# Scores and the packed projection as float32 matmuls on 64x32 array tiles instead of block-diagonal 128-row matmuls

## The chip, the cores and the metric

The kernel runs on one core of one Trainium2 chip. The core has a matrix engine (TensorE, PE in the profile, with its weight loads shown apart as PEld), a vector engine (VectorE, DVE), a scalar engine (ScalarE, ACT), a general engine (GpSimd, POOL) and a queue engine that here only starts DMAs (SyncE, SP). They work in parallel and wait for each other through semaphores. Matrix results land in PSUM, an accumulator memory of which the kernel uses eight banks and from which ScalarE and VectorE read them; operands lie in SBUF, both of 128 partitions. The metric is the device time of one execution in microseconds (us). Three runs of the kernel before took 1118.48, 1119.23 and 1120.44 us; the median is 1119.23.

## The reference

The reference first packs each head's sequence with 32 learned queries, attends to the packed result, and puts the output through two dense blocks. Cut to what matters (4 batches, 8 heads, 576 positions, head size 64, 32 packed positions):

```python
def sm_attn(qq, kk, vv):                       # softmax(qq kk^T / 8) vv
    s = scale * np.matmul(qq, kk.transpose(0, 1, 3, 2))
    a = np.exp(s - np.max(s, axis=-1, keepdims=True))
    return np.matmul(a / (np.sum(a, axis=-1, keepdims=True) + 1e-09), vv)

p_packed = sm_attn(p, k, v)                    # 32 rows for each head
x = sm_attn(q, p_packed, p_packed)             # heads side by side: 2304 x 512
for e in range(4):                             # w1[e] 512x1024, w2[e] 1024x512
    out += prob[:, e:e+1] * (np.maximum(x @ w1[e], 0.0) @ w2[e])
h = out @ w_in                                 # w_in 512x2048, float64
return (h - np.tanh(h)) @ w_out                # w_out 2048x512, float64
```

## The kernel before

The work runs in two phases. Phase A is the attention and the first mixture; phase B, from about 690 us, is the second dense block and is not touched by the change. Tokens are handled in two halves p = 0, 1 of two batches each (nine tiles of 128 tokens), and the mixture in eight chunks c of 512 hidden columns.

Large products are kept accurate by splitting an operand x into a rounded high part and the rest, both of type fp32r, and adding three matmuls (high by high, high by low, low by high). A plain float32 matmul needs no split. Both kinds are used.

The stages have letters, and the order in which the program creates them is written out by hand in the strings START_A, START_B (the start and chunk 0), EVEN, ODD and LAST (the later chunks). From that order and its own estimates a scheduler makes the order of each engine.

- K, V, L load k, v and q of a batch. S (`pack_scores`, L157) makes the scores of the 32 packed queries of two head pairs against all 576 keys, and the softmax. Two heads share the 128 rows of the array: `pbd` holds the packed queries block-diagonally, each pair as 128x64 with zeros in the off-diagonal blocks, so one float32 matmul on a 64-column strip gives two heads. T (L183) transposes the probabilities, P (`pack_pv`, L195) multiplies them with v and copies the result, 32 packed rows a head, into a block-diagonal buffer `ppbd` (eight copies of 64x32 a batch). Z splits `ppbd` into `pph` and `ppl`.
- Q (`q_scores`, L221) makes the scores of two token tiles against the packed rows, again with a block-diagonal operand, then a softmax in groups of 32: maximum (qmx), subtraction, exponential (ScalarE), sum (qsm), two small steps, multiplication. X (`q_T`, L261) transposes the probabilities and splits them into `a2h` and `a2l`.
- W (`pack_w1`, L348) is the packed projection. Instead of applying the probabilities to the packed rows and then w1, the packed rows are multiplied with a chunk of w1 first, and the probabilities are applied to that. Each call takes two head pairs: six fp32r matmuls (L355) of 512 columns from the splits of `ppbd` and of w1, then three ScalarE passes (`wph`, L365) and three VectorE passes (`wpl`, L368). There are 4 calls a chunk, 32 in all. The tile w1 is staged by `a0`, split by `b0` (`w1h`, `w1l`, L341).
- u (`up`, L374; the accumulator is hps) applies the probabilities to that product, with the ReLU; d (`down`, L405; yps) multiplies with w2 and adds the weighted result to x. An underscore decodes a piece of the float64 weights of phase B in the background.

The accumulators come from two pools: `ps2`, two buffers of two banks, used by S, T, W, u and later by phase B, and `ps1`, four buffers of one bank, used by P, Q, X and d. A stage that needs a buffer waits until the engines that read the stage before it in that buffer are done.

## Time and profile before

| | before |
|---|---|
| median of three runs, us | 1119.23 (1118.48 to 1120.44) |
| span of the profiled execution, us | 1116.0 |
| TensorE busy, of the span | 1097.5 us (98%) |
| VectorE busy | 766.3 us (69%) |
| ScalarE busy | 521.0 us (47%) |
| GpSimd busy | 11.9 us (1%) |
| chain that ended last | PE 97%, DVE 2% |
| share of W on that chain | 4% |
| shares of pv, sc, qsc on it | 1% each |

The profile shows one execution. The span goes from its first to its last instruction; its own time outside of that is not listed apart, and the median of the runs is 3.2 us longer than the span. Busy times are of instructions, so a matmul counts from its start to the modelled end of its last column, and successive ones overlap: what one costs in a stream is the distance between two starts, not its duration. A float32 matmul appears as two instructions, an fp32r matmul as one. The chain that ended last is followed back from the last instruction, at each step to what released it.

### The profile page before, as it was taken

How to read it: one execution, taken by the hardware profiler on the slowest of the kernel's cores; microseconds unless marked ns; L12 is line 12 of the kernel's file. 1: busy time of each engine (PE TensorE's matmuls, PEld its weight loads, DVE VectorE, ACT ScalarE, POOL GpSimd, SP SyncE). 2: the span in 40 equal slices, each digit the busy share in tenths (PEclk: the TensorE clock that was granted, in tenths of full speed). 3: DMA queues.
4: the chain of work that ended last, by engine and by line, in shares of the span. 5: the costliest groups of instructions: out<-in, count | busy, mean ns of one | idle time of the engine just before them, and what ended most of it. 6: DMA issues, size and time to landing. Idle time of an engine off the chain costs nothing.

```text
span 1116.0 us, 14894 instructions
## 1 busy us (share of the span) xinstructions
PE 1097.5 (98%) x6100; PEld 937.7 (84%) x6100; DVE 766.3 (69%) x1055; ACT 521.0 (47%) x743; POOL 11.9 (1%) x13
## 2 busy tenths in 40 slices
PE   7799999999999999999999999999999999999998
PEld 5688888898888888888889888888888888888887
DVE  5937456876876776867787544487676767777775
ACT  3535533433434433443434322476666556556463
POOL 2100000000000000000000000000000000000000
PEclk9999999999999999999999999999999999999999
DMA  9620202322331331332322031201011262202102
GB/s 341 227 86 1 76 22 93 114 95 76 113 113 66 114 124 57 115 112 84 107 95 95 19 145 64 95 1 38 1 38 38 74 228 95 76 1 76 57 19 76
DMA packets 33668, 96.68 MB, mean 87 GB/s; under 512 B 3776, under 2 KB 3776, under 8 KB 33600
## 3 DMA queue, kind: packets, MB, share of 16 engines
q1 hardware_dynamic: 33600, 95.73, 24.6%
q8 instruction: 48, 0.79, 0.3%
q14 instruction: 20, 0.16, 0.0%
HBM read 69.51 MB, written 26.21 MB: 86 GB/s over the span
## 4 chain that ended last, share of the span: by engine, by line
PE 97%; DVE 2%; ACT 0%; DMA 0%; issue 0%; DVEq 0%; SPq 0%; ACTq 0%
PE yps L413 35%; PE hps L387 18%; PE ops L626 18%; PE h3ps L570 18%; PE wps L355 4%; PE pv L205 1%; PE sc L162 1%; PE xps L448 1%; PE qsc L235 1%; DVE wpl L368 0%; PE tp L188 0%; PE qtp L268 0%; DMA kt<-in_kT_dram 0%; DVE mx L168 0%; DVE pn L464 0%
## 5 line engine op out<-in xcount | busy, mean ns | idle before, releaser
L413 PE MATMUL yps<-w2h,hm 128*128 128x512 f32 x640 | 206.2, 391 | 0.0
L570 PE MATMUL h3ps<-xh,ws 128*128 128x512 f32 (+1 forms) x640 | 187.3, 368 | 0.0
L626 PE MATMUL ops<-ws,gh 128*128 128x512 f32 x576 | 177.2, 396 | 0.0
L413 PE MATMUL yps<-w2h,hu 128*128 128x512 f32 x512 | 165.0, 392 | 0.0
L387 PE MATMUL hps<-a2h,wph 128*128 128x256 f32 (+1 forms) x512 | 151.3, 296 | 2.5 <-DVE wpl L368 1.7
L387 PE MATMUL hps<-a2l,wph 128*128 128x256 f32 (+1 forms) x512 | 151.5, 296 | 1.0 <-DVE a2l L272 1.0
L387 PE MATMUL hps<-a2h,wpl 128*128 128x256 f32 (+1 forms) x512 | 151.3, 296 | 0.0
L413 PEld LDWEIGHTS yps<-w2h,hm 128*128 128x128 f32 x640 | 119.8, 188 | 23.5
L570 PEld LDWEIGHTS h3ps<-xh,ws 128*128 128x128 f32 x640 | 116.5, 188 | 20.6
L626 PEld LDWEIGHTS ops<-ws,gh 128*128 128x128 f32 x576 | 107.6, 189 | 24.2 <-ACT gh L605 0.2
L413 PE MATMUL yps<-w2l,hm 128*128 128x512 f32 x320 | 125.1, 391 | 0.0
L424 DVE SCALAR_TENSOR_TENSOR x<-yps,pn,x 128x512 f32<-128x512 f32 x126 | 93.7, 747 | 37.7 <-PE yps L413 36.5
L570 PE MATMUL h3ps<-xl,ws 128*128 128x512 f32 (+1 forms) x320 | 117.7, 368 | 0.0
L397 DVE SCALAR_TENSOR_TENSOR hm<-hps,hm 128x640 fp32r<-128x640 f32 x64 | 52.7, 823 | 85.7 <-ACT hm L396 85.3
L626 PE MATMUL ops<-ws,gl 128*128 128x512 f32 x288 | 109.7, 395 | 0.0
L413 PEld LDWEIGHTS yps<-w2h,hu 128*128 128x128 f32 x512 | 94.5, 188 | 16.9
L396 ACT ACTIVATE hm<-hps 128x640 fp32r<-128x640 f32 x64 | 45.1, 705 | 135.4 <-PE hps L387 135.2
L387 PEld LDWEIGHTS hps<-a2h,wph 128*128 128x128 f32 x512 | 96.9, 189 | 7.4 <-issue 2.1
L387 PEld LDWEIGHTS hps<-a2l,wph 128*128 128x128 f32 x512 | 96.9, 189 | 4.8 <-DVE a2l L272 1.2
L396 ACT ACTIVATE hu<-hps 128x512 fp32r<-128x512 f32 x64 | 38.2, 597 | 131.8 <-PE hps L387 131.6
L413 PE MATMUL yps<-w2l,hu 128*128 128x512 f32 x256 | 99.6, 391 | 0.0
L368 DVE TENSOR_TENSOR wpl<-wps,wph 64x512 fp32r<-64x512 f32 (+1 forms) x96 | 80.5, 865 | 26.7 <-ACT wph L365 25.9
(99 smaller groups left out, 1598.8 us busy)
## 6 DMA issues: line engine op xcount, KB each, us to landing
st<-in_w_dram SPq DMA_DIRECT2D x32, 512.0 KB, 3.8
f<-in_win_dram SPq DMA_DIRECT2D x16, 512.0 KB, 4.1
f<-in_wout_dram SPq DMA_DIRECT2D x16, 512.0 KB, 3.8
win<-fo SPq DMA_DIRECT2D x16, 512.0 KB, 2.9
wout<-fo SPq DMA_DIRECT2D x16, 512.0 KB, 2.9
ws<-win SPq DMA_DIRECT2D x16, 512.0 KB, 4.6
ws<-wout SPq DMA_DIRECT2D x16, 512.0 KB, 4.8
kt<-in_kT_dram SPq DMA_DIRECT2D x16, 288.0 KB, 6.2
```

Source lines behind the costliest of these rows:

```text
L162: nc.tensor.matmul(out=sc[64 * jj:64 * jj + 64, h, 0:288], lhsT=pbd[:, 4 * b + j, :], rhs=kv_k[b][j][:, 288 * h:288 * h + 288],)
L205: nc.tensor.matmul(out=pv[64 * h:64 * h + 64, jj, :], lhsT=kv_v[b][c][0:n, 128 * j + 64 * h:128 * j + 64 * h + 64], rhs=a1t[:, c, k0:k0 + ...
L235: nc.tensor.matmul(out=sc[r - r0:r - r0 + 64, o:o + 64], lhsT=qs[2 * p + bi][j][:, r - bi * S_LEN:r + 64 - bi * S_LEN], rhs=ppbd[p][:, j, ...
L355: nc.tensor.matmul(out=ps[:, jj], lhsT=a[p][:, j, :], rhs=w[c, g][:, jj], start=(n == 0), stop=(n == 2),)
L368: nc.vector.tensor_tensor(out=l[o], in0=ps[i], in1=f(h[o]), op=ALU.subtract)
L387: nc.tensor.matmul(out=ps[:, ff, 0:n], lhsT=a[c, p, g][:, bi, c0:c0 + 128], rhs=x[p][:, g, t0:t0 + n], start=(k == 0), stop=(k == 5),)
L396: last[1] = nc.scalar.activation(out=hi[:, :, d], in_=ps[:, :, 0:n], func=ACTF.Relu).ins
L397: last[0] = nc.vector.scalar_tensor_tensor(out=lo[:, :, d], in0=ps[:, :, 0:n], scalar=0.0, in1=f(hi[:, :, d]), op0=ALU.max, op1=ALU.subtra ...
L413: nc.tensor.matmul(out=ps, lhsT=a[:, ff, o:o + 128], rhs=w[c, fp][:, ff], start=(k == 0), stop=(k == 11),)
L424: last[0] = nc.vector.scalar_tensor_tensor(out=x2[tt], in0=ps, scalar=pn[:, tt, e:e + 1], in1=x2[tt], op0=ALU.mult, op1=ALU.add,).ins
L570: nc.tensor.matmul(out=ps[:, ff, 0:n], lhsT=w[:, wl, kd, :], rhs=x[:, kd, :], start=(k == 0), stop=(k == 11),)
L626: nc.tensor.matmul(out=ops[u][t], lhsT=a[ff][:, d], rhs=w[:, wl], start=(i == 0 and ff == 0 and k == 0), stop=(i == 3 and ff == 1 and k == 2),
```

## The change

`pack_scores` now takes a whole batch. The packed queries are kept as they were loaded (`pst`: head parity r = 0 in rows 0 to 63, r = 1 in rows 64 to 127), and each of the eight heads is a float32 matmul of 64 rows by 32 columns: head pair j on column strip j, parity r on row half r, with an accumulator buffer of its own for each parity. `pack_pv` writes one tile of 128x32 for each head pair (`ppd`, without zeros), in one ScalarE copy instead of eight copies. `q_scores` does for each parity what it did for two, on 64x64 tiles, into a buffer of `ps2` instead of `ps1`. `pack_w1` takes one batch and all four head pairs: eight float32 matmuls of 512 columns on the eight tiles, no splits, one pass each on ScalarE and VectorE. The splits of w1 (on GpSimd in chunk 0, on ScalarE and VectorE later), of `ppbd`, and the clearing of the block-diagonal buffers go. `pack_T` moves from `ps2` to two buffers of `ps1`. The tokens of the strings are adapted, otherwise their order is that of before.

```diff
-    "S00 S01 S02 T00 S03 T01 P00 T02 P01 T03 b000 P02 P03 Z0 b001 a100 a101 "
+    "S00 S01 T00 T01 T02 P00 T03 P01 Z0 a100 a101 "
...
-    p_w1 = pool("w1", 4, pa)
+    p_w1 = pool("w1", 2, pa)
     p_st = pool("st", 2, pa)
     p_f64 = pool("f64", 1, pa)
     p_fo = pool("fo", 1, pa)
     p_pp = pool("pp", 2, pa)
-    pbd = p_pp.tile([128, 4 * B, 64], F32, name="pbd", bufs=1)
+    pst = p_pp.tile([128, 4 * B, 32], F32, name="pst", bufs=1)
     ps2 = pool("ps2", 2, space=PSUM)
     ps1 = pool("ps1", 4, space=PSUM)
...
-    def pack_scores(b, g):
-        sc = ps2.tile([128, 2, 512], F32, tag="p2", name="sc")
-        for jj in range(2):
-            j = 2 * g + jj
-            for h in range(2):
-                nc.tensor.matmul(
-                    out=sc[64 * jj:64 * jj + 64, h, 0:288],
-                    lhsT=pbd[:, 4 * b + j, :],
-                    rhs=kv_k[b][j][:, 288 * h:288 * h + 288],
-                )
...
+    def pack_scores(b):
+        scs = [ps2.tile([128, 2, 512], F32, tag="p2", name="sc") for _ in range(2)]
+        for h in range(2):
+            for j in range(4):
+                for r in range(2):
+                    d = slice(64 * r, 64 * r + 64)
+                    nc.tensor.matmul(
+                        out=scs[r][32 * j:32 * j + 32, h, 0:288],
+                        lhsT=pst[d, 4 * b + j, :],
+                        rhs=kv_k[b][j][d, 288 * h:288 * h + 288],
+                    )
...
-        tp = ps2.tile([128, 2, 4, 128], F32, tag="p2", name="tp")
+        tp = ps1.tile([128, 4, 128], F32, tag="p1", name="tp")
+        te = ps1.tile([128, 128], F32, tag="p1", name="te")
...
-        for jj in range(2):
-            j = 2 * g + jj
-            c0 = 64 * (bi ^ jj)
-            nc.scalar.activation(
-                out=ppbd[b // 2][0:64, j, c0:c0 + 32], in_=pv[0:64, jj, :], func=ACTF.Copy
-            )
-            nc.vector.tensor_copy(
-                out=ppbd[b // 2][64:128, j, c0 + 32:c0 + 64], in_=pv[64:128, jj, :]
-            )
+        nc.scalar.activation(out=ppd[p][:, bi], in_=pv, func=ACTF.Copy)
...
     def q_scores(p, t0):
         nt = min(2, TP - t0)
-        n = 256 * nt
-        sc = ps1.tile([128, 512], F32, tag="p1", name="qsc")
+        sc = ps2.tile([128, 2, 512], F32, tag="p2", name="qsc")
         for i in range(nt):
-            r0 = (t0 + i) * 128
-            for bi in range(2):
-                lo, hi = max(r0, bi * S_LEN), min(r0 + 128, (bi + 1) * S_LEN)
-                if lo >= hi:
-                    continue
-                for blk in range(4):
-                    j = blk ^ bi
-                    o, c0 = 256 * i + 64 * blk, 64 * (blk & 1)
-                    for r in range(lo, hi, 64):
+            for j in range(4):
+                for k in range(2):
+                    x = (t0 + i) * 128 + 64 * k
+                    bi, s0 = x // S_LEN, x % S_LEN
+                    for r in range(2):
+                        d = slice(64 * r, 64 * r + 64)
+                        o = 128 * i + 32 * j
                         nc.tensor.matmul(
-                            out=sc[r - r0:r - r0 + 64, o:o + 64],
-                            lhsT=qs[2 * p + bi][j][:, r - bi * S_LEN:r + 64 - bi * S_LEN],
-                            rhs=ppbd[p][:, j, c0:c0 + 64],
+                            out=sc[64 * k:64 * k + 64, r, o:o + 32],
+                            lhsT=qs[2 * p + bi][j][d, s0:s0 + 64],
+                            rhs=ppd[p][d, bi, j, :],
                         )
...
-    def pp_init(p):
-        ppbd[p] = u2t([128, 4, 128], F32, "ppbd")
-        nc.gpsimd.memset(ppbd[p], 0.0)
-
-    def pp_split(p):
-        pph[p] = p_pp.tile([128, 4, 128], F32R, tag="pph", name="pph")
-        ppl[p] = p_pp.tile([128, 4, 128], F32R, tag="ppl", name="ppl")
-        split(pph[p], ppl[p], ppbd[p])
+    def a2_init(p):
...
     def stage(kind, c, g):
-        src = w1 if kind == 0 else w2
-        t = p_st.tile([128, 2, 512], F32, tag="st", name="st")
-        nc.sync.dma_start(out=t, in_=src[c, :, 2 * g:2 * g + 2, :])
-        staged[kind, c, g] = t
-    def prep_w1(c, g):
-        w1h[c, g] = p_w1.tile([128, 2, 512], F32R, tag="w1", name="w1h")
-        w1l[c, g] = p_w1.tile([128, 2, 512], F32R, tag="w1", name="w1l")
-        split(w1h[c, g], w1l[c, g], staged.pop((0, c, g)), nc.gpsimd if c == 0 else None)
+        if kind == 0:
+            t = w1f[c, g] = p_w1.tile([128, 2, 512], F32, tag="w1", name="w1f")
+        else:
+            t = staged[c, g] = p_st.tile([128, 2, 512], F32, tag="st", name="st")
+        nc.sync.dma_start(out=t, in_=(w1, w2)[kind][c, :, 2 * g:2 * g + 2, :])
...
-    def pack_w1(c, p, g):
+    def pack_w1(c, p, bi):
         ps = ps2.tile([128, 2, 512], F32, tag="p2", name="wps")
-        for jj in range(2):
-            j = 2 * g + jj
-            for n, (a, w) in enumerate(
-                ((pph, w1h), (pph, w1l), (ppl, w1h))
-            ):
+        for j in range(4):
+            for r in range(2):
+                d = slice(64 * r, 64 * r + 64)
                 nc.tensor.matmul(
-                    out=ps[:, jj], lhsT=a[p][:, j, :], rhs=w[c, g][:, jj],
-                    start=(n == 0), stop=(n == 2),
+                    out=ps[32 * j:32 * j + 32, r, :],
+                    lhsT=ppd[p][d, bi, j, :], rhs=w1f[c, j // 2][d, j % 2, :],
                 )
-        h = p_wp.tile([128, 2, 512], F32R, tag="wph", name="wph")
-        l = p_wp.tile([128, 2, 512], F32R, tag="wpl", name="wpl")
-        parts = []
-        for rows, bi, jj, n in ((slice(0, 64), 0, 0, 2), (slice(64, 128), 0, 1, 1), (slice(64, 128), 1, 0, 1)):
-            o = (rows, slice(bi, bi + n))
-            i = (rows, slice(jj, jj + n))
-            nc.scalar.activation(out=h[o], in_=ps[i], func=ACTF.Copy)
-            parts.append((o, i))
-        for o, i in parts:
-            nc.vector.tensor_tensor(out=l[o], in0=ps[i], in1=f(h[o]), op=ALU.subtract)
-        wph[c, p, g], wpl[c, p, g] = h, l
+        h = wph[c, p, bi] = p_wp.tile([128, 2, 512], F32R, tag="wph", name="wph")
+        l = wpl[c, p, bi] = p_wp.tile([128, 2, 512], F32R, tag="wpl", name="wpl")
+        nc.scalar.activation(out=h, in_=ps, func=ACTF.Copy)
+        nc.vector.tensor_tensor(out=l, in0=ps, in1=f(h), op=ALU.subtract)
```

What the change does to the order is shown at three places. The first is TensorE in chunk 1, at W of p = 1 (wps is the accumulator of W, yps that of d); the kernel before:

```order
L413 MATMUL yps<-w2h,hm 128x512 x2
L355 MATMUL wps<-w1h,pph 128x512
L355 MATMUL wps<-w1l,pph 128x512
L355 MATMUL wps<-w1h,ppl 128x512
L355 MATMUL wps<-w1h,pph 128x512
L355 MATMUL wps<-w1l,pph 128x512
L355 MATMUL wps<-w1h,ppl 128x512
L413 MATMUL yps<-w2l,hm 128x512
L413 MATMUL yps<-w2h,hm 128x512
```

The same place after:

```order
L387 MATMUL yps<-w2h,hm 128x512 x2
L336 MATMUL wps<-w1f,ppd 32x512 x8
L387 MATMUL yps<-w2l,hm 128x512
L387 MATMUL yps<-w2h,hm 128x512
L336 MATMUL wps<-w1f,ppd 32x512 x8
L387 MATMUL yps<-w2h,hm 128x512
L387 MATMUL yps<-w2l,hm 128x512
```

Six matmuls with splits as operands have become eight of 32 rows in the same place, with two rows of yps between one W and the next.

The second place is TensorE in chunk 0 where the q scores of p = 1 begin (qsc; qtp are the transposes X, pv the end of P); the kernel before, from the last pv on:

```order
L205 MATMUL pv<-a1e,vt 64x32 x2
L235 MATMUL qsc<-ppbd,qt 64x64 x32
L413 MATMUL yps<-w2h,hm 128x512
L413 MATMUL yps<-w2l,hm 128x512
L413 MATMUL yps<-w2h,hm 128x512 x2
L413 MATMUL yps<-w2l,hm 128x512
L355 MATMUL wps<-w1h,pph 128x512
L355 MATMUL wps<-w1l,pph 128x512
L355 MATMUL wps<-w1h,pph 128x512
L355 MATMUL wps<-w1l,pph 128x512
```

After, from the last pv on:

```order
L210 MATMUL pv<-a1e,vt 64x32 x2
L229 MATMUL qsc<-ppd,qt 64x32 x64
L336 MATMUL wps<-w1f,ppd 32x512 x8
L387 MATMUL yps<-w2h,hm 128x512
L387 MATMUL yps<-w2l,hm 128x512
L387 MATMUL yps<-w2h,hm 128x512 x2
L387 MATMUL yps<-w2l,hm 128x512
```

and on from the second W:

```order
L387 MATMUL yps<-w2h,hm 128x512 x2
L336 MATMUL wps<-w1f,ppd 32x512 x8
L387 MATMUL yps<-w2l,hm 128x512
L387 MATMUL yps<-w2h,hm 128x512
L262 MATMUL qtp<-ident,a_1220 128x128 x2
L229 MATMUL qsc<-ppd,qt 64x32 x32
L262 MATMUL qtp<-ident,a_1220 128x128 x2
L387 MATMUL yps<-w2h,hu 128x512
```

Before, half as many matmuls make Q10 and Q11, and W stands in pieces between them and yps; after, Q10 and Q11 are followed at once by a whole W, then ten instructions of yps, the other W, two transposes and Q12.

The third place is VectorE at the same stage (a_1150 and a_1177 are the probabilities of Q10 and Q11 before, a_1220 and a_1263 after); the kernel before:

```order
L246 TENSOR_TENSOR a_1150<-qsc,qmx 128x512
L243 TENSOR_REDUCE qmx<-qsc 128x16
L246 TENSOR_TENSOR a_1177<-qsc,qmx 128x512
L251 TENSOR_REDUCE qsm<-a_1150 128x16
L252 TENSOR_SCALAR qsm<-qsm 128x16
L251 TENSOR_REDUCE qsm<-a_1177 128x16
L255 RECIPROCAL qsm<-qsm 128x16
L252 TENSOR_SCALAR qsm<-qsm 128x16
L256 TENSOR_TENSOR a_1150<-a_1150,qsm 128x512
L255 RECIPROCAL qsm<-qsm 128x16
L256 TENSOR_TENSOR a_1177<-a_1177,qsm 128x512
L243 TENSOR_REDUCE qmx<-qsc 128x16
```

After:

```order
L241 TENSOR_TENSOR a_1220<-qsc,qmx 128x512
L246 TENSOR_REDUCE qsm<-a_1220 128x16
L247 TENSOR_SCALAR qsm<-qsm 128x16
L250 RECIPROCAL qsm<-qsm 128x16
L251 TENSOR_TENSOR a_1220<-a_1220,qsm 128x512
L238 TENSOR_REDUCE qmx<-qsc 128x16
L241 TENSOR_TENSOR a_1263<-qsc,qmx 128x512
L246 TENSOR_REDUCE qsm<-a_1263 128x16
L247 TENSOR_SCALAR qsm<-qsm 128x16
L250 RECIPROCAL qsm<-qsm 128x16
L251 TENSOR_TENSOR a_1263<-a_1263,qsm 128x512
L343 TENSOR_TENSOR wpl<-wps,wph 128x1024 x2
```

Before, the steps of the two softmaxes alternate; after, those of Q10 all stand ahead of those of Q11, and the two passes on W behind both.

## Rows read from the trace of the kernel before

**Rows 1.** Busy time by stage: stretch, length, each engine's busy us (instructions), clock, DMA.

```profile
0.00:42.00 42.00, 28.25 (x344) 20.25 (x344) 27.94 (x65) 17.98 (x37) 7.20 (x11) 1.00 0.99 345
42.00:140.00 98.00, 97.55 (x822) 83.50 (x823) 54.89 (x115) 47.78 (x84) 4.75 (x2) 1.00 0.19 60
140.00:690.00 550.00, 550.00 (x2968) 484.05 (x2966) 386.62 (x563) 209.69 (x315) 0.00 (x0) 1.00 0.27 92
690.00:1116.00 426.00, 421.72 (x1971) 349.95 (x1969) 296.85 (x316) 245.50 (x309) 0.00 (x0) 1.00 0.17 60
```

**Rows 2.** The chain around one W: start us, us, what.

```profile
175.02 1.36 PE wps L355 x6
176.38 0.45 PE yps L413 x2
```

**Rows 3.** TensorE timeline and line 162, scores: start us, us; durations in ns.

```profile
9.91 0.47 PE L162 MATMUL sc<-kt,pbd 128*64 128x288 f32 x2 [0.99 <-ACT a L173]
9.91 1.20 PE L162 MATMUL sc<-kt,pbd 128*64 128x288 f32 x8 [0.99 <-ACT a L173]
L162 PE MATMUL sc<-kt,pbd x64: 406/406/740, 4.3 to 67.5; 128*64 128x288 f32 x64
```

**Rows 4.** TensorE timeline, from 128-column matmuls to a 64-column shape.

```profile
92.56 0.39 PE L413 MATMUL yps<-w2h,hm 128*128 128x512 f32 x1
92.88 0.45 PE L235 MATMUL qsc<-ppbd,qt 128*64 128x64 f32 x4
```

**Rows 5.** TensorE timeline of q scores and back to 128 columns; line 235.

```profile
87.01 2.09 PE L235 MATMUL qsc<-ppbd,qt 128*64 128x64 f32 x64
88.52 0.58 PE L235 MATMUL qsc<-ppbd,qt 128*64 128x64 f32 x14
89.03 0.50 PE L413 MATMUL yps<-w2h,hm 128*128 128x512 f32 x1
89.36 0.39 PE L413 MATMUL yps<-w2l,hm 128*128 128x512 f32 x1
L235 PE MATMUL qsc<-ppbd,qt x288: 219/222/271, 22.7 to 108.4; 128*64 128x64 f32 x144
```

**Rows 6.** Busy time by stage of line 355 (W): PE, PEld.

```profile
42.00:140.00 98.00, 6.06 (x24) 4.43 (x24) 1.00 0.19 60
140.00:690.00 550.00, 38.77 (x156) 29.28 (x156) 1.00 0.27 92
```

**Rows 7.** The same of line 162 (scores).

```profile
42.00:140.00 98.00, 3.59 (x24) 1.64 (x24) 1.00 0.19 60
```

**Rows 8.** Lines 368, 113, 114: instructions, min/median/max ns, first and last start.

```profile
L368 DVE TENSOR_TENSOR wpl<-wps,wph x96: 686/695/1218, 32.8 to 664.0; 64x512 fp32r<-64x512 f32 x64, 64x1024 fp32r<-64x1024 f32 x32
L113 ACT ACTIVATE w1h<-st x16: 1043/1053/1055, 19.0 to 605.2; 128x1024 fp32r<-128x1024 f32 x16
L114 DVE TENSOR_TENSOR w1l<-st,w1h x14: 1211/1217/1227, 116.3 to 607.4; 128x1024 fp32r<-128x1024 f32 x14
```

**Rows 9.** Timeline of the start, and the first hps on the chain.

```profile
24.55 1.03 PE L235 MATMUL qsc<-ppbd,qt 128*64 128x64 f32 x26 [0.30 <-DMA qt<-in_qT_dram]
26.79 0.69 DVE L114 TENSOR_TENSOR ppl<-ppbd,pph 128x512 fp32r<-128x512 f32 x1 [0.69 <-ACT pph L113]
27.51 0.69 DVE L243 TENSOR_REDUCE qmx<-qsc 128x16 f32<-128x512 f32 x1
28.24 0.69 DVE L246 TENSOR_TENSOR a<-qsc,qmx 128x512 f32<-128x512 f32 x1
28.96 0.63 ACT L249 ACTIVATE a<-a 128x512 f32<-128x512 f32 x1 [2.21 <-DVE a L246]
31.45 0.68 DVE L243 TENSOR_REDUCE qmx<-qsc 128x16 f32<-128x512 f32 x1
40.54 0.75 DVE L168 TENSOR_REDUCE mx<-sc 128x1 f32<-128x576 f32 x1
42.45 1.70 PE hps L387 x12
```

More of the change, by code (lines that the diff above doesn't have):

```diff
@@ L114, in split @@
         (eng or nc.vector).tensor_tensor(out=lo, in0=src, in1=f(hi), op=ALU.subtract)
-    ppbd, pph, ppl, a2h, a2l = {}, {}, {}, {}, {}
+    ppd, a2h, a2l = {}, {}, {}
     a1s, a1ts, a2s = {}, {}, {}
@@ L192, in pack_T, with pack_pv @@
-        nc.vector.tensor_copy(out=a1e[0:64], in_=tp[0:64, 1, 0])
-        a1ts[b, g] = (a1t, a1e)
-    def pack_pv(b, g):
-        a1t, a1e = a1ts.pop((b, g))
-        bi = b % 2
-        pv = ps1.tile([128, 2, 32], F32, tag="p1", name="pv")
-        for jj in range(2):
-            j = 2 * g + jj
+        nc.scalar.activation(out=a1t, in_=tp, func=ACTF.Copy)
+        nc.vector.tensor_copy(out=a1e[0:64], in_=te[0:64])
+        a1ts[b, r] = (a1t, a1e)
+    def pack_pv(b):
+        ts = [a1ts.pop((b, r)) for r in range(2)]
+        p, bi = b // 2, b % 2
+        if bi == 0:
+            ppd[p] = p_pp.tile([128, 2, 4, 32], F32, tag="ppd", name="ppd")
+        pv = ps1.tile([128, 4, 32], F32, tag="p1", name="pv")
+        for j in range(4):
@@ L201, in pack_pv @@
             for c in range(5):
                 n = 128 if c < 4 else 64
-                for h in range(2):
-                    k0 = 64 * jj + 32 * h
+                for r, (a1t, a1e) in enumerate(ts):
+                    c0 = 128 * j + 64 * r
+                    k0 = 32 * j
                     nc.tensor.matmul(
-                        out=pv[64 * h:64 * h + 64, jj, :],
-                        lhsT=kv_v[b][c][0:n, 128 * j + 64 * h:128 * j + 64 * h + 64],
+                        out=pv[64 * r:64 * r + 64, j, :],
+                        lhsT=kv_v[b][c][0:n, c0:c0 + 64],
@@ L246, in q_scores @@
+        a2 = u2t([128, 2, 256], F32, "a2")
+        a24 = a2[:, :, 0:n].rearrange("p r (g k) -> p r g k", k=32)
         nc.vector.tensor_tensor(
-            out=a23, in0=sc3, in1=mx[:, 0:G].to_broadcast([128, G, 32]), op=ALU.subtract
+            out=a24, in0=sc4, in1=mx[:, :, 0:G].to_broadcast([128, 2, G, 32]), op=ALU.subtract
         )
-        nc.scalar.activation(out=a2[:, 0:n], in_=a2[:, 0:n], func=ACTF.Exp, scale=0.125)
-        sm = small.tile([128, 16, 1], F32, tag="qsm", name="qsm")
```

91 lines of the change are left out of this document (42 added, 49 removed), and 8 rows, old and new, of the table START_B.

## The prediction, made before the changed kernel was run

> **What bounds the kernel now.** I read the busy time by stage first [rows 1]. In 140 to 690 us TensorE is busy for 550.00 of 550 us and in 690 to 1116 us for 421.72 of 426, at a granted clock of 1.00; VectorE has 386.62 of 550 in the first of these, ScalarE 209.69. From 42 to 140 us TensorE is busy 97.55 of 98. Only the first 42 us leave it free (28.25 busy). So after 42 us an edit is worth what it changes in TensorE's own instruction stream, plus any wait that it puts into that stream. Before 42 us the end is set by the DMA that brings the q tiles and by VectorE, and an edit is worth what it does to the moment when the first large matmuls (hps) start. The rest of my reading is therefore single TensorE rows (how long one packed projection takes, what a change of tile shape costs) and the VectorE chain of the start.
>
> **The packed projection W.** Before, a call is six fp32r matmuls of 512 columns: 1.36 us on the chain [rows 2], 0.227 us each. After, it is eight float32 matmuls on eight array tiles (four column strips by two row halves). What one costs comes from the scores of before, which are float32 on two column strips of 64. Their matmul is recorded as two instructions. Two instructions together take 0.47 us, eight take 1.20 us [rows 3], so each further pair takes (1.20 - 0.47) / 3 = 0.243 us for 288 columns. The program order there is two matmuls on strip 0 and then two on strip 1; that they finish in four pair steps says that the strips run side by side and that each strip works through its own instructions. A 512-column instruction then takes 0.243 x 512 / 288 = 0.43 us, and a matmul 0.86 us on its tile. If all eight tiles run together the body is 0.86 us plus what it takes to load the first tile and to start the others. The first pair is 0.06 longer than the 0.41 of one instruction [rows 3], for a load of 64 columns and one other strip; I estimate 0.03 for a load of 32 columns and 0.04 for seven other tiles.
>
> Around the body the shape of the array changes twice, which before did not happen. Entering a 64-column shape: 92.56 to 92.88 is 0.32 us [rows 4], where 0.227 is the stream, so 0.09 more. Leaving it: 14 instructions of qsc begin at 88.52 and end at 89.10, the last of them began 0.22 earlier, at 88.88, and the first yps stands at 89.03 [rows 5]: 0.15, of which 0.054 (0.243 x 64 / 288) is the stream of 64 columns, so 0.10 more. That yps takes until 89.36, 0.33 instead of 0.227, another 0.10 for a weight load that nothing hides. So a call costs 0.09 + 0.03 + 0.86 + 0.04 + 0.10 + 0.10 = 1.22 us against 1.36. Six matmuls each, 24 + 156 of them stand after 42 us [rows 6]: 30 calls, **-4.2 us**. Two thirds of what the tiles save is given back by the two changes of shape. No row shows four column strips or two row halves at once, so the ends are far apart: with everything side by side and the starts free, -5.4 us; with the strips sharing one stream of operands, so that only half run at full rate, the body is 1.72 and the 30 calls cost +21.6 us. I take the value nearest to the rows, where a second strip cost nothing.
>
> Here a page speaks against the change. The Trainium skill, "TensorE: Matmul & The Clock Gate", section "Part 3: Packing small matmuls — row/col tiling", says that matmuls start and end strictly in program order and only weight loads are pulled ahead. By that rule the second half of each float32 matmul would hold up the next tile: nine steps of 0.43 us, a call of 4.2 us, and with 30 calls some 1205 us (the last case below). The trace disagrees: in strict order the eight instructions of [rows 3] would need seven starts with only one overlap, 0.24 x 6 + 0.41 = 1.9 us, and they took 1.20.
>
> **Scores.** 24 instructions (three of the eight blocks of four matmuls) stand after 42 us [rows 7]. Three blocks of 4 x 0.243 are 2.9 us, with some 0.2 for loads. After, a batch is 16 matmuls on eight tiles; the fourth batch alone stands after 42 us, as two runs of eight on four tiles, four steps of 0.243 each: 1.95 us and some 0.15 for loads. **-1.0 us**, and one change of shape fewer, **-0.3**. If strips share a stream: +1.9 instead.
>
> **q scores.** Twice the matmuls at half the columns: for two token tiles 32 instead of 16. Before, 64 instructions in 2.09 us, (2.09 - 0.22) / 31 = 0.060 per pair [rows 5]. After, 128 instructions on four tiles (two row halves, two column halves) are 32 steps again; at 0.060 the same time, **0**. The rows give no separate price of 32 columns; the other bound, row halves one after another, doubles the two thirds that stand after 42 us: 96 steps more, +5.8 us.
>
> **The evacuation and the splits.** wph was three ScalarE passes a call, wpl two VectorE passes of 0.695 and one of 1.218, 2.61 us; they become one pass each of 128x1024, for which the splits of w1 give 1.05 and 1.22 [rows 8]. With those splits gone too, VectorE loses 14 x 1.22 + 32 x 1.39 = 61 us, and ScalarE its 16 x 1.05 and two passes a call. I cost that at **nothing** after 42 us: TensorE waits for neither there, yps matmuls cover it, and nothing becomes late when it goes. W also gives its accumulator buffer back sooner.
>
> **The wait that is added.** The q scores move from the pool of four one-bank buffers to the pool of two two-bank buffers, where W and hps also live. The order of TensorE after shows where that bites: Q10 and Q11 (64 matmuls) take both buffers, then W, ten instructions of yps, W, two transposes, and then Q12. VectorE's order changes too: before, the softmaxes of Q10 and Q11 are interleaved; after, Q10's seven steps run through, then Q11's. One such chain takes 31.45 - 27.51 = 3.94 us, its maximum and subtraction 0.69 each, the exponential 0.63 [rows 9]. With Q10 starting at 0: it is done at 0.95, subtracted at 2.35; TensorE reaches W at 1.9 and waits 0.5. Q11 is subtracted at 0.95 + 3.94 + 1.4 = 6.3; TensorE, after W (1.2) and ten yps (2.3), is there at 5.9 and waits 0.4. Q12 wants W's buffer. The first wph stands on ScalarE behind Q11's exponential, and the first wpl on VectorE behind the whole chain of Q11, at 8.9 to 10.1; TensorE is there at 8.4 and waits 1.7. Everything behind Q12 on TensorE's queue (yps, hps) is held with it. At u001 the same pool costs some 0.5 (Q04 waits for the evacuation of hps). Sum 3.1, **+3.0 us**; ends 1 (VectorE early) and 9.6, if each of the eight q-score blocks after the first two costs 1.2.
>
> **The first 42 us.** Removed on VectorE before the first hps: ppl at 0.69 [rows 9], twice 1.39 on wpl, and eight small copies into ppbd: some 4.9 us. The two GpSimd splits of w1 beside it go too. But Q00 cannot finish before the fourth q tile, for which TensorE waited until 24.55 [rows 9], and the scheduler now puts more ahead of the first hps: both halves of the third batch's scores, and X01 and X02. On VectorE that is a maximum of 0.75 [rows 9], two a2l of the subtraction's size (1.4), 0.65 of standing idle for an exponential that no other step fills now, and about 1 us of small steps: 3.8 us; and ScalarE's two exponentials of the scores must give the buffers back before hps. Chaining these durations from Q00's end I get the first two hps groups done 1.7 us later than before, where the second began at 42.45 [rows 9], with 2.1 us of TensorE work (eight transposes, half a batch of scores) already behind it: a gain of 0.4. If all 4.9 removed were gained it would be 5; if the 3.8 added were simply paid, a loss of 3. I take **-1.0**.
>
> **Sum.** -4.2 - 1.0 - 0.3 + 0 + 3.0 - 1.0 = -3.5 us. The span of 1116.0 becomes 1112.5; about 3.2 us lie around it, since the runs' median is 1119.23, so **1115.8 us**.
>
> **Rivals.**
> - *Strips share the operand stream* (slower). W and scores at half rate: 1115.8 + 30 x 0.86 + 1.9 = 1143.5. For it: four strips with different float32 operands from the same partitions are read nowhere in the trace. Against it: two strips cost no more than one. It decides as soon as the body of W passes 1.0 us.
> - *The two-bank pool becomes the bound of the first 140 us.* Stalls of 9.6 instead of 3.0: 1122.4. For it: VectorE's order puts whole softmax chains ahead of evacuations. Against it: yps from the other pool fills most gaps.
> - *The start gains all that VectorE loses.* 4 us more: 1111.8. For it: VectorE is the chain from 27.5 to 42 us. Against it: the q DMA and the larger set of work ahead of hps.
> - *Strict order*, so that the tiles do not run side by side at all: the change would not do what it says, 1205 us.
>
> **How the numbers follow.** My forecast has 0.62, with 1112 to 1120 as its own range; shared stream 0.13; pool stalls 0.12; the start 0.10; strict order 0.03. The range 1110 to 1130 leaves out the two heavy cases (0.16) but for some partial sharing, and the edges of the others. 0.2% is 2.2 us, about what a measurement of this kernel tells from no change: faster means below 1117.0, slower above 1121.5. The forecast lies below 1117.0 with some 0.62 of its weight and above 1121.5 with 0.05; with the start on the fast side, pool stalls split between same and slower, and both heavy cases slower: 0.48 faster, 0.26 same, 0.26 slower.
>
> **What would show it.** Right: between two yps around W, 1.2 to 1.25 us instead of 1.36, with eight tiles' starts within 0.1 us; gaps of 0.3 to 2 us on TensorE before W and Q12 near 85 to 100 us, released by VectorE; 140 to 690 us shorter by about 4 with no idle time. Wrong: starts of W's tiles 0.4 us apart, a W above 1.4 us, idle time on TensorE after 140 us, or a first hps more than 4 us from where it was.

## The result, and the profile after

The changed kernel takes 1131.17 us (median of four runs, 1128.49 to 1132.41) against 1119.25 for the kernel before on the same chip: ratio 1.0102, 95% interval 1.0086 to 1.0119. It is 1.0% slower where I forecast 0.3% faster, and 1.2 us beyond the upper end of my range. Its profiled execution spans 1130.6 us. One execution of the variant `e_cover`, the profiled one, ran at a mean granted clock of 0.556 and took 1818.09 us; its time is left out, and no trace of that variant is read.

Busy time by stage of the changed kernel, columns as in [rows 1]:

```profile
0.00:42.00 42.00, 32.59 (x407) 21.21 (x408) 13.14 (x41) 8.86 (x18) 0.71 (x6) 1.00 0.84 292
42.00:140.00 98.00, 90.36 (x1060) 73.71 (x1058) 53.35 (x102) 36.72 (x62) 4.74 (x2) 0.97 0.24 72
140.00:690.00 550.00, 550.00 (x3264) 459.03 (x3263) 344.48 (x494) 172.87 (x257) 0.00 (x0) 1.00 0.26 91
```

Against [rows 1]: VectorE has 42 us less to do from 140 to 690 us and TensorE is as full as before; from 42 to 140 us TensorE now stands idle for 7.6 us and its granted clock is 0.97; and in the first 42 us TensorE is *busier* (32.6 for 28.3) although it gets less far (its first hps comes at 52.36 us, before at 38.73). Milestones tell where the 14.6 us between the two spans arise. Both are single executions: the span of the changed kernel is the longest of its four (1126.7 to 1130.6), and that of the kernel before is shorter than any of the 37 spans on record beside the variants (1116.4 to 1119.8, median 1117.8), so the 14.6 us stand for 11.9 by the medians. The milestones are start times of TensorE matmuls in the timelines (hps counted one by one; h3ps is the accumulator of the first product of phase B); the last two columns are the span and the median of the runs:

```
kernel                       hps 1   hps 25  hps 193  first h3ps   span     median
before                       38.73   47.63   146.07    708.65    1116.0    1119.25
changed                      52.36   59.34   164.15    723.23    1130.6    1131.17
s_alone  (before + S,T,P)    51.03   59.29   158.24    720.81    1128.2    1129.35
w_alone2 (before + W)        39.91   49.26   146.10    705.15    1112.6    1113.05
s_undone (changed - S,T,P)   38.65   48.00   149.00    708.08    1115.5    1118.06
e_warm   (10 dense)          45.26   53.78   157.07    716.15    1123.5    1125.00
e_warm2  (16 dense)          46.40   53.03   156.42    715.51    1122.9    1124.63
e_warm3  (and S10 later)     41.78   53.34   154.34    713.43    1120.8    1123.36
e_best   (w_alone2 + dense)  37.54   46.59   143.15    702.21    1109.6    1110.86
e_order  (S10 later)         47.13   61.23   161.47    720.56    1127.9    1128.27
e_pre    (3 dense)           55.18   62.92   168.51    727.57    1134.9    1134.19
e_cover_d (below)            37.97   51.46   147.28    706.36    1114.0    1116.23
```

From the 193rd hps to the first h3ps the changed kernel needs 559.1 us where before needed 562.6: the 26 calls of W in that stretch bring 3.5 us, as forecast. Phase B, behind it, is 407.4 in both. The loss arises ahead of that: +13.6 us at the first hps, +11.7 at the 25th, +18.1 at the 193rd.

The W that brings the gain, on TensorE's timeline (start us, us, engine, line, operation), beside [rows 2]:

```profile
234.24 0.40 PE L387 MATMUL yps<-w2h,hm 128*128 128x512 f32 x1
234.56 1.09 PE L336 MATMUL wps<-w1f,ppd 64*32 64x512 f32 x16
235.58 0.50 PE L387 MATMUL yps<-w2h,hm 128*128 128x512 f32 x1
```

Sixteen instructions on eight tiles take 1.02 us from their first start to the next yps; with 0.10 on the way in (0.32 where a plain step is 0.227) and 0.10 for the uncovered weight load behind, a call costs 1.22. The trace has the eight first instructions start within 0.047 us of each other (234.563 to 234.610), the second ones from 235.017. The Trainium skill, "TensorE: Matmul & The Clock Gate", "Part 3: Packing small matmuls — row/col tiling", has matmuls of all tiles start and end in program order. The program has one matmul for each tile here, and each is recorded as two instructions, of which the second ones all start after all the first ones; if a matmul's two instructions stand next to each other in program order, which the trace does not tell, the trace disagrees, as [rows 3] did.

And the start, where the loss is:

```profile
4.47 1.17 PE L163 MATMUL sc<-kt,pst 64*32 64x288 f32 x4 [4.47 <-DMA kt<-in_kT_dram]
6.07 3.85 PE L163 MATMUL sc<-kt,pst 64*32 64x288 f32 x28 [0.42 <-DMA kt<-in_kT_dram]
12.42 2.87 PE L163 MATMUL sc<-kt,pst 64*32 64x288 f32 x32 [2.50 <-ACT a L175]
27.00 1.96 PE L336 MATMUL wps<-w1f,ppd 64*32 64x512 f32 x16
46.48 4.16 PE L163 MATMUL sc<-kt,pst 64*32 64x288 f32 x32
52.72 0.41 PE L361 MATMUL hps<-a2l,wph 128*128 128x256 f32 x1
55.63 0.28 PE L361 MATMUL hps<-a2h,wph 128*128 128x256 f32 x1
```

The same sixteen instructions of W take 1.96 us here and 1.09 at 234 us; hps takes 0.41 up to 55.3 us and 0.28 from 55.6. So TensorE runs at its 1.2 GHz level from its first matmul to 55 us, and the rise comes 3 us into the dense 128x128 hps. In the kernel before the long durations end at 7.7 us (the maximum of 740 ns in [rows 3] is from there, the median 406 is at 2.4 GHz). The column of the granted clock does not show this: it reads 1.00 in the first 42 us of both, because the first change of the clock that each trace records is the rise itself, at 55.5 us here and at 7.7 us before, and the column takes what is ahead of the first record as full. The other three executions of the changed kernel have mean granted clocks of 0.979, 0.980 and 0.985 where the profiled one has 0.997; at half the rate that is, by estimate, 34 to 47 us at the low level in each of them. The column does show two later falls (columns as above):

```profile
66.00:69.00 3.00, 3.00 (x12) 2.71 (x11) 1.68 (x5) 0.70 (x1) 0.00 (x0) 0.50 0.11 45
82.00:86.00 4.00, 4.00 (x83) 3.28 (x81) 0.00 (x0) 0.69 (x1) 0.00 (x0) 1.00 0.00 0
86.00:89.00 3.00, 3.00 (x13) 2.38 (x12) 0.00 (x0) 0.28 (x1) 0.00 (x0) 0.54 0.61 187
```

The first follows an idle gap of 2.04 us, the second 80 instructions of pv with no gap at all (82.90 to 86.26). Each lasts some 3.4 us, in which an hps takes 0.267 us instead of 0.149 and a yps 0.427 instead of 0.227, and so costs some 1.6 us. The end of the pv and the first yps behind it:

```profile
85.37 0.66 PE L210 MATMUL pv<-a1t,vt 128*64 128x32 f32 x16
85.95 0.30 PE L210 MATMUL pv<-a1e,vt 64*64 64x32 f32 x4
86.19 0.78 PE L387 MATMUL yps<-w2h,hm 128*128 128x512 f32 x1
```

### The profile page after: what moved, and what is told of

Its sections match the earlier page's. It is cut to its first block, busy times and chain, and to the rows that moved or that the text cites. A ratio compares the mean times of both kernels' runs of the same rounds, so it can differ in the third digit from the quotient of the medians.

```text
span 1130.6 us, 15997 instructions
## 1 busy us (share of the span) xinstructions
PE 1109.3 (98%) x6772; PEld 916.6 (81%) x6772; DVE 713.6 (63%) x958; ACT 467.0 (41%) x648; POOL 5.4 (0%) x8
## 4 chain that ended last, share of the span: by engine, by line
PE 95%; DVE 3%; ACT 1%; issue 0%; DMA 0%; DVEq 0%; SPq 0%; ACTq 0%
PE yps L387 35%; PE hps L361 18%; PE ops L594 18%; PE h3ps L538 17%; PE wps L336 3%; PE pv L210 2%; PE sc L163 1%; PE xps L422 1%; PE qsc L229 0%; DMA kt<-in_kT_dram 0%; DVE a L241 0%; PE qtp L262 0%; DVE qsm L246 0%; PE tp L191 0%; DVE a L251 0%
## 5 line engine op out<-in xcount | busy, mean ns | idle before, releaser
L387 PE MATMUL yps<-w2h,hm 128*128 128x512 f32 x640 | 209.6, 396 | 0.0
L361 PEld LDWEIGHTS hps<-a2h,wpl 128*128 128x128 f32 x512 | 98.0, 191 | 0.1
```

Source lines behind the costliest of these rows:

```text
L361: nc.tensor.matmul(out=ps[:, ff, 0:n], lhsT=a[c, p, bi][:, g, c0:c0 + 128], rhs=x[p][:, g, t0:t0 + n], start=(k == 0), stop=(k == 5),)
L387: nc.tensor.matmul(out=ps, lhsT=a[:, ff, o:o + 128], rhs=w[c, fp][:, ff], start=(k == 0), stop=(k == 11),)
```

## The experiments

Theory 1, the clock: with first scores on 64x32 tiles and the waits behind them TensorE stays at 1.2 GHz through the start. Theory 2, the waits: the pool `ps2`, which Q, W and scores in one piece now fill, and the later softmaxes cost the time.

**One part at a time.** `s_undone` is the changed kernel with S, T and P of before (... stands for lines left out):

```diff
-    "S00 S01 T00 T01 T02 P00 T03 P01 Z0 a100 a101 "
+    "S00 S01 S02 T00 S03 T01 P00 T02 P01 T03 P02 P03 Z0 a100 a101 "
...
-        nc.scalar.activation(out=ppd[p][:, bi], in_=pv, func=ACTF.Copy)
+        nc.scalar.activation(out=ppd[b // 2][:, bi, 2 * g:2 * g + 2, :], in_=pv, func=ACTF.Copy)
```

> The changed kernel with the first attention's scores, transposes and products of the kernel before (block-diagonal 128x64 stationary operand, two blocks of heads at a time), while the query scores and the projection stay on 64x32 tiles. Theory 1 (the clock: with the first scores on 64x32 tiles and the waits between them, TensorE stays at its 1.2 GHz level until about 55 us): the first scores are dense again, matmuls run at the short durations from about 8 us on, the first up-projection starts at 39 to 41 us instead of 52.4, and the time is 1112 to 1118 us, below both kernels by the 4 us that the projection gains. Theory 2 (the loss is in the new waits: query scores and projection share the pool ps2, and the softmax of the query scores comes late on DVE): the first up-projection still starts after 48 us and the time is 1125 to 1131 us.

Measured 1118.06 us (1117.47 to 1122.01), ratio to before 0.9992 (0.9983 to 1.0001); the first hps at 38.65. So 13.1 us of the loss hang on the form of S, T and P. The first hps is where theory 1 has it (0.35 us sooner), and the time stands 0.06 us above its range: the gain of W is not there.

`s_alone` is its mirror, the kernel before with only S, T and P changed (pv is copied into the block-diagonal buffer as before).

> The kernel before with only the first scores, transposes and products of the changed kernel (64x32 tiles, one head parity per half of the rows, a batch in one piece); query scores and projection stay block-diagonal split passes. Theory 1 (clock): TensorE's durations stay at the 1.2 GHz level until the first dense 128x128 work, the first up-projection starts some 8 to 13 us later than the 38.7 us of before, and the time is 1127 to 1133 us. Theory 2 (the waits of query scores and projection in ps2): none of these is in this kernel, so the time is within 3 us of 1119 us.

Measured 1129.35 us, ratio 1.0086 (1.0071 to 1.0101); first hps at 51.03. As theory 1 has it: these three stages alone cost some 10 us, without any query score in `ps2`. By itself this does not part the clock from scores in one piece: the first hps also waits here, 2.19 us for the exponential of the scores (ScalarE).

`w_alone` is the kernel before with only W on tiles; for it `ppbd` is laid out by head pair, which also halves the copies of P:

```diff
...
-                    lhsT=a[p][:, j, :], rhs=w[c, g][:, jj],
+                    out=ps[32 * j:32 * j + 32, r, :],
+                    lhsT=ppbd[p][d, bi, j, 32 * r:32 * r + 32], rhs=w1f[c, j // 2][d, j % 2, :],
```

> The kernel before with only the packed projection on 64x32 tiles (no splits of w1 and of the packed values); first scores as before and query scores still block-diagonal 128x64 in the pool ps1. Both theories: the start is as before, the projection gains what its two kinds of call differ by, (1.36 - 1.22) us for each of 32 calls, 4 us in all: 1113 to 1117 us. Against the variant with query scores on tiles it prices these: theory 1 has the two within 2 us, theory 2 has this one 8 us or more below.

Measured 1214.25 us, a miss that says nothing on either theory. The waits of TensorE in its trace (engine, line, waited for: us in total, times, longest) name the cause:

```profile
PE h3ps L546 <- DMA ws<-win: 95.6, 1, 95.6
```

I had left `ppbd` in the pool that the decode of the float64 weights uses; W now reads it to the last chunk. In `w_alone2` it has a pool of its own.

> The variant with only the projection on tiles again, with the packed values of each pair of batches in a pool of their own. In the first form they lay in the pool u2, whose 22 buffers the decode of the float64 weights needs too, and as the projection now reads them to the last chunk, two buffers stayed taken: that decode came late and the second mixture waited 96 us for it. Both theories: with that gone the projection's gain of (1.36 - 1.22) us for each of 30 calls is left, less what the clock or the waits of the first calls take: 1114 to 1118 us. Theory 2 (new ps2 waits of the query scores) has it 3 us or more below the variant with query scores on tiles (1118.1 us); theory 1 has them within 2 us.

Measured 1113.05 us, ratio 0.9942 (0.9929 to 0.9956), some 1 us below the range of both theories. W alone is worth its forecast and more: 6.6 us by the medians, against 1119.61 for the kernel before beside it, and 6.6 by the medians of all spans too (1111.25 against 1117.8). The two traces differ by 3.4 only: profiled were the longest of four here (1112.6; the others 1110.9 to 1111.4) and, of the kernel before, one shorter than all 13 beside it. And it is 5.0 us below `s_undone`, which differs from it by Q on tiles in `ps2` (and by how P is copied out): here theory 2 is right on the difference. TensorE in `s_undone`, idle time and its releaser in brackets:

```profile
91.02 1.09 PE L333 MATMUL wps<-w1f,ppd 64*32 64x512 f32 x16 [0.71 <-DVE a L238]
94.95 1.09 PE L333 MATMUL wps<-w1f,ppd 64*32 64x512 f32 x16 [0.34 <-DVE a L238]
98.61 1.14 PE L226 MATMUL qsc<-ppd,qt 64*64 64x32 f32 x64 [1.68 <-DVE wpl L340]
```

**The clock by itself.** `e_warm` adds dense matmuls (token D, accumulator dps) to the changed kernel, each held at its place in TensorE's order:

```diff
+    def dense(n):
...
+            ps = ps1.tile([128, 512], F32, tag="p1", name="dps")
+            for _ in range(n):
+                pe[0] = nc.tensor.matmul(out=ps, lhsT=dz[:, 0:128], rhs=dz)
...
-    "S00 S01 T00 T01 T02 P00 T03 P01 Z0 a100 a101 "
+    "D3 S00 D2 S01 D1 T00 T01 D1 T02 P00 T03 P01 Z0 a100 a101 "
-    "W000 Q00 Q01 X00 K2 ...
+    "W000 Q00 D1 Q01 D1 X00 D1 K2 ...
```

> The changed kernel with eleven added dense float32 matmuls of 128x128 by 512 columns on a tile of zeros in the first 40 us (three before the first scores, the others in the gaps between scores, transposes and query scores); nothing reads their result, and all else is the same. They cost TensorE 0.85 us each at the full rate. Theory 1 (clock): with them TensorE reaches the full rate before the first scores and holds it for most of the start; the first up-projection begins at 43 to 47 us instead of 52.4 and the time is 1119 to 1126 us in spite of the added work. Theory 2 (waits and order): the added work comes on top, the first up-projection stays at 51 us or later, and the time is 1130 to 1138 us.

Measured 1125.00 us (1121.73 to 1125.36), ratio to before 1.0041 (1.0027 to 1.0055): 6.2 us *below* the changed kernel with ten matmuls more (the strings have D3, D2 and five D1; the expectation counts eleven), as theory 1 has it and theory 2 excludes. `e_warm2` has sixteen, not the eighteen of its expectation: six further ones, one inside each P and two around S10.

> The changed kernel with eighteen dense float32 matmuls of 128x128 by 512 columns spread over the start, one inside each product of the packed attention too and two around the scores of the second pair. In the variant with eleven the short durations held from 6.8 to 26.9 us and again from 36.9 us, and were lost for 26.9 to 36.9 and 45.3 to 50.6 us. Theory 1 (clock; what holds it is a dense 128x128 matmul now and then): the short durations hold from 7 us on without a break, the scores, query scores and projections all run at the short durations, the first up-projection begins at 41 to 44 us, and the time is 1118 to 1124 us though 15 us of matmuls at the full rate's 0.85 us were added. Theory 2: the seven further matmuls only add their time: 1126 to 1132 us.

Measured 1124.63 us, ratio 1.0048 (1.0033 to 1.0064), 0.6 us above the range of theory 1 and below that of theory 2. The granted clock of the same stretches, first of `e_warm`, then of `e_warm2`:

```profile
12.00:27.00 15.00, 14.01 (x232) 9.67 (x224) 6.23 (x23) 4.62 (x11) 0.00 (x0) 1.00 1.05 344
27.00:37.00 10.00, 10.00 (x144) 6.53 (x142) 6.09 (x10) 2.94 (x5) 0.00 (x0) 0.50 1.04 377
46.00:51.00 5.00, 5.00 (x26) 5.00 (x25) 2.93 (x8) 2.03 (x4) 0.00 (x0) 0.52 0.00 0
```

```profile
27.00:37.00 10.00, 7.79 (x182) 4.29 (x188) 5.61 (x9) 2.42 (x4) 0.00 (x0) 1.00 1.04 372
46.00:51.00 5.00, 3.40 (x25) 2.99 (x26) 3.50 (x10) 2.57 (x7) 0.00 (x0) 1.00 0.00 0
```

The rate holds as expected, but the first hps came at 46.4, not at 41 to 44: TensorE waits there for something else (below). So the six further matmuls hold the rate for two more stretches and bring 0.4 us. `e_pre` has only the first three dense matmuls.

> The changed kernel with only the three dense matmuls ahead of the first scores. Theory 1a (once at the full rate, TensorE keeps it as long as its work has no gap of some us): the first scores run at the short durations, and so does what follows, and the time is 1122 to 1126 us, as with eleven. Theory 1b (64x32-tile scores and the waits behind them lose it again): short durations for the first scores only, long ones again from the second scores or the transposes on, up to the dense up-projection: first up-projection at 50 to 52 us, 1128 to 1131 us.

Measured 1134.19 us, ratio 1.0129 (1.0112 to 1.0146). Theory 1b on the rate, and 3.2 us above it in time, which is a wait of another kind. The scheduler put the sum over the mixture weights `pn` (psum) ahead of the copy a1e (of T) on VectorE; VectorE stood idle 3.85 us for the load of `pn`, the copy came late, and the transpose that needs its buffer waited 3.15 us:

```profile
21.90 0.23 DVE L436 TENSOR_REDUCE psum<-pn 128x18 f32<-128x72 f32 x1 [3.85 <-DMA pn<-in_dp_dram]
22.10 0.28 DVE L196 COPY a1e<-te 64x128 f32<-64x128 f32 x1
22.43 0.42 PE L192 MATMUL te<-ident,a 128*64 128x128 f32 x1 [3.15 <-DVE a1e L196]
```

In the changed kernel psum stands behind that copy and waits 0.81 us. So an added matmul can shift the order of other engines too, and the times of these variants are not the clock alone. What the run does show: here the fall is recorded, with durations equal to those of the changed kernel (2.87 us for the same 32 instructions), so these are the 1.2 GHz level (scores, then two stretches of the clock):

```profile
8.58 1.16 PE L164 MATMUL sc<-kt,pst 64*32 64x288 f32 x20 [0.71 <-DMA kt<-in_kT_dram]
12.24 2.87 PE L164 MATMUL sc<-kt,pst 64*32 64x288 f32 x32 [2.50 <-ACT a L176]
```

```profile
12.00:27.00 15.00, 10.84 (x111) 7.75 (x111) 5.68 (x23) 4.03 (x11) 0.00 (x0) 0.51 1.05 362
51.00:60.00 9.00, 8.01 (x46) 6.25 (x43) 6.84 (x18) 3.41 (x7) 0.00 (x0) 0.50 0.13 43
```

**The scores in one piece.** `e_order` moves one step of the changed kernel:

```diff
-... Q02 X01 S10 u000 V2 ...
+... Q02 X01 u000 S10 V2 ...
```

> The changed kernel with one step moved: the first scores of the second pair (S10) stand behind the first up-projection (u000) instead of in front of it. In the changed kernel these scores, in one piece, take both buffers of ps2 at 46.5 us, and the up-projection behind them starts at 52.4 us. Theory 1 (the clock is all of the loss in the start): the up-projection starts about 5 us sooner, and as it is the first dense work, the full rate comes back that much sooner, but scores and their waits still have to be done behind it: 1126 to 1129 us. Theory 2 (the wait for the two buffers is a loss of its own): the wait is not only moved but goes, 1123 to 1126 us. Neither: 1130 to 1132 us.

Measured 1128.27 us, ratio 1.0077 (1.0063 to 1.0090): theory 1's figure. In its trace the first hps comes at 47.13 and the rate rises at 52.5 us, 3.0 sooner than in the changed kernel; the 25th hps comes later (61.23 for 59.34), and the time is won behind it, where this trace has one fall of the clock, at 110.5 us, and that of the changed kernel two. `e_warm3` moves the same step in `e_warm2`.

> The variant with dense matmuls spread over the whole start (1124.6 us, all durations at the full rate from 7 us on) with the same step moved, S10 behind u000 (and without the dense matmul between them). In its trace the up-projection starts at 46.4 us, after scores on both buffers of ps2, though its own operands were there by about 40 us. The clock is the same in both, so any difference is the wait: theory 2 (a wait for ps2 beside the clock) has the first up-projection at 41 to 43 us and the time at 1120 to 1122.5 us; theory 1 alone has 1124 to 1126 us.

Measured 1123.36 us (1122.58 to 1126.18) against 1124.57 to 1126.3 of `e_warm2`: the ranges overlap, and the time lies between the two expectations. S10 and the first hps of `e_warm2`, then the first hps of `e_warm3` and where the wait went:

```profile
41.06 2.21 PE L164 MATMUL sc<-kt,pst 64*32 64x288 f32 x32
46.40 0.39 PE L367 MATMUL hps<-a2h,wph 128*128 128x256 f32 x1 [1.06 <-ACT a L176]
```

```profile
41.78 0.39 PE L367 MATMUL hps<-a2h,wph 128*128 128x256 f32 x1
46.36 1.72 PE L164 MATMUL sc<-kt,pst 64*32 64x288 f32 x32
49.99 0.67 PE L235 MATMUL qsc<-ppd,qt 64*64 64x32 f32 x32 [1.48 <-ACT a L176]
```

The first hps comes 4.6 us sooner, as theory 2 has it, but the 25th does not (53.34 for 53.03): the scores hold both buffers against the next Q instead. The wait is real and was mostly moved; the spans differ by 2.1 us. The clock is not quite the same in both, as the expectation had it: the trace of `e_warm3` has a fall from 35.6 to 39.0 us that `e_warm2` has not, so the 4.6 us are, if anything, too few.

**The waits of Q, and a faster version.** `e_cover` moves d between Q and W in `s_undone` (and d000 between Q04 and Q03):

```diff
-... Z1 Q10 Q11 W010 W011 d006 Q12 X10 d007 d008 u010 ...
+... Z1 Q10 Q11 d006 W010 d007 W011 X10 Q12 d008 u010 ...
```

> The variant with the old first scores and with query scores and projection on tiles (1118.1 us), with down-projections of the first pair moved between the query scores and the projections of the second pair (Q10 Q11 d006 W010 d007 W011 X10 Q12 d008, and d000 between Q04 and Q03). Its trace has TensorE idle there for 0.7, 0.35 and 1.7 us and before that for 0.3 and 0.8 us, on the two buffers of ps2. If these waits are what eats the projection's gain: 1114 to 1116 us. If the clock in the start (long durations from 29.7 to 40.3 us) is all of it: 1117.5 to 1119 us.

Measured 1116.66 us, ratio to before 0.9975 (0.9965 to 0.9985; `s_undone` had 0.9992): between the two expectations, 1.4 us. So covering these waits gives back 1.4 of the 5.0 us. `e_cover_d` adds two dense matmuls, ahead of Q01 and inside it.

> The variant with the covered waits and two dense float32 matmuls of 128x128 by 512 columns, put into the waits of the query scores for their transfers at 26.1 and 28.5 us, where TensorE is idle for 1.4 and 0.9 us. Theory 1 (clock): the projection and the query scores behind them run at the short durations, which gives back about 2 to 3 us: 1111 to 1115 us, 2 us or more below the variant without them. Theory 2: no difference, or 1 us more.

Measured 1116.23 us, ratio 0.9968 (0.9956 to 0.9981): theory 1 missed. The rate does hold at 1.00 from 8.2 us on, and buys nothing: in this stretch TensorE waits for VectorE's softmaxes anyway (gaps of 0.5, 1.2 and 1.5 us between 31 and 42 us). Its trace has no wait left at W and Q12 near 90 us. `e_best` puts four into the longest gap of `w_alone2`:

```diff
-    "W000 Q00 Q01 X00 K2 W001 I1 n Q02 ...
+    "W000 Q00 Q01 W001 D4 X00 K2 I1 n Q02 ...
```

> The variant with only the projection on tiles (1113.05 us) and four dense float32 matmuls of 128x128 by 512 columns put into its longest idle time of TensorE, 5.4 us from 28.6 to 34.0 us, in which it waits for DVE's softmax of the query scores. In its trace the durations behind that gap are the long ones up to 44.4 us. Theory 1 (clock): they are short now and the time falls by 1 to 3 us, to 1110 to 1112 us. Theory 2 (the chain over DVE and ACT sets the start): within 0.7 us of 1113 us.

Measured 1110.86 us (1110.07 to 1111.34), ratio to before 0.9919 (0.9907 to 0.9932), against 0.9942 (0.9929 to 0.9956) of `w_alone2`: the fastest here, 2.2 us below. The edit moves W001 ahead of X00 as well, but on TensorE it stood there already (27.52 us in `w_alone2`, 27.47 here). The two timelines, `w_alone2` first; the gap remains, shorter by the dense matmuls, and what follows it runs in 0.58 of the time:

```profile
33.97 1.09 PE L260 MATMUL qtp<-ident,a 128*128 128x128 f32 x4 [5.36 <-DVE qsm L244]
34.99 2.46 PE L227 MATMUL qsc<-ppbd,qt 128*64 128x64 f32 x32
```

```profile
28.49 3.70 PE L484 MATMUL dps<-dz 128*128 128x512 f32 x8
33.92 0.63 PE L261 MATMUL qtp<-ident,a 128*128 128x128 f32 x4 [1.72 <-DVE qsm L245]
34.47 1.43 PE L228 MATMUL qsc<-ppbd,qt 128*64 128x64 f32 x32
```

## Why the prediction was wrong

**The step that failed is "The first 42 us": -1.0 us forecast, +11.7 us at the 25th hps.** I chained durations that the kernel before shows at 2.4 GHz, after taking away the dense scores that had brought it there (with them back, in `s_undone`, the recorded rise is at 9.6 us). Each TensorE step of that chain takes up to twice as long in the changed kernel (S10 4.16 us where I had 1.95 and some 0.15 for loads, and where `e_warm2` has 2.21 at the same place), and nothing in my rivals was about the clock: all four are about tiles, pools and VectorE. Restoring the rate gives back 6.5 us by the medians (`e_warm2`) and 6.3 at the 25th hps, net of the dense matmuls, so the clock's share is about that or more. A smaller part is a wait I did not price: S10 in one piece takes both buffers of `ps2` in front of the first hps, which then waits for the exponential that frees one (1.06 us in `e_warm2`, 1.57 in `e_warm`); what it is worth in the changed kernel was not measured by itself. The prediction's own sign of being wrong, a first hps more than 4 us from where it was, came true.

By the two traces, with the terms that the prediction has behind 42 us put behind the 25th hps, the sum comes out so. Up to the 25th hps: -1.0 forecast, +11.7. From there to the 193rd: +1.1 forecast (waits 3.0, scores and shapes -1.3, four calls of W -0.6), +6.4. The other 26 calls of W: -3.6 forecast, -3.5. Phase B: no change forecast, none measured.

**The added waits** were right one by one and short in sum: 0.49, 0.35 and 1.73 us before W, W and Q12 (forecast 0.5, 0.4, 1.7), all for VectorE as named; but 2.04 at u001 for a forecast of 0.5, and two falls of the clock, some 1.6 us each, that I did not have. The rival with 9.6 us of pool stalls did not come; by the medians Q in `ps2` costs 5.0 us (`s_undone` against `w_alone2`) for the 3.0 of my sum. The four waits in the changed kernel:

```profile
65.01 0.39 PE L361 MATMUL hps<-a2h,wph 128*128 128x320 f32 x1 [2.04 <-DVE a L241]
106.09 1.09 PE L336 MATMUL wps<-w1f,ppd 64*32 64x512 f32 x16 [0.49 <-DVE a L241]
110.02 1.09 PE L336 MATMUL wps<-w1f,ppd 64*32 64x512 f32 x16 [0.35 <-DVE a L241]
113.73 1.14 PE L229 MATMUL qsc<-ppd,qt 64*64 64x32 f32 x64 [1.73 <-DVE wpl L343]
```

**W** was right: 1.22 us a call. Strict order is excluded by the eight starts, a shared operand stream by the 1.02 us of the body (I had 1.72 for it). **Q** was near its 0: 126 instructions in 2.29 us, [rows 5] has 64 in 2.09. **Scores**: a batch takes 1.90 us at the full rate, as worked out, but not at the rate that it got, and two batches instead of one stand behind 42 us in the changed kernel. In the rival of the shared stream, the +1.9 for scores is what is added to the -1.0, not what stands in its place; the 1143.5 us use it so. A batch in `e_warm2`:

```profile
11.44 1.90 PE L164 MATMUL sc<-kt,pst 64*32 64x288 f32 x32 [0.58 <-ACT a L176]
```

Removing VectorE and ScalarE work was worth nothing later, as forecast: from 140 to 690 us TensorE is busy for 550.00 of 550 us with that work and without it, and the 3.5 us of that stretch are W's.

From one variant to the next the medians go -6.6 (`w_alone2`), +5.0 (Q in `ps2`), +13.1 (S, T, P), in sum +11.5 from the 1119.61 of the kernel before beside `w_alone2`. That these steps add up is no test, since each begins where the last ended; a test of its own is `s_alone`, where S, T and P cost 9.7 without the other two parts. What is not settled: why `w_alone2` gains 6.6 us where 30 calls at the 0.135 us of the trace make 4; what makes the rest of the 5.0 us (`e_cover_d`, at 1.00 throughout and without the waits at W and Q12, is still 3.2 us above `w_alone2`); and how the 13.1 split further, since the dense matmuls that restore the rate cost time themselves: `e_warm2` is still 11.6 us above `w_alone2`, 10.3 by the two traces, of which 3.8 arise up to the 25th hps and 6.5 between the 25th and the 193rd, as waits for `ps2` and as two dense matmuls on the path.

## What to carry to other kernels

Durations in a trace are valid for the clock under which they were taken: where a change removes dense matmuls or puts waits among them, price what follows at both levels, 1.2 and 2.4 GHz, before adding it up. Packing small matmuls onto tiles pays in a stream of dense work and can cost more than it saves at a start that depends on dense work to raise the clock; so change the one (W) and leave the other (the first scores), and put an idle gap to use with dense work where the stages behind it wait for TensorE (`e_best` gained 2.2 us) and not for another engine (`e_cover_d` gained nothing). A buffer count is part of the price of doing a stage in one piece.

## What the runs showed of the hardware that I had not expected

- TensorE can lose its full rate with no idle gap: in `e_warm` it falls at 26.75 us, after pv, W and qsc since 18.05 us with five transposes among them and no gap above 0.43 us, and reads 0.50 for 27 to 37 us with TensorE busy for 10.00 of 10; in the changed kernel it falls behind 80 instructions of pv in a row (lines above). With one dense 128x128 matmul inside each P it stays at 1.00 (`e_warm2`). The Trainium skill, "TensorE: Matmul & The Clock Gate", "Why this matters for your kernels", warns of idle gaps between bursts; this trace has the fall without one.
- The granted-clock column can read 1.00 while matmuls take the durations of the 1.2 GHz level, ahead of the first change that the trace records: the start of the changed kernel (to 55.5 us) and of `s_alone` (to 36.0). Durations of one shape, early and late, tell it.
